# Idle products at the start, one weight piece a slot, another order of the value products, and later sums of weight factors

## The chip, the core and the metric

The kernel runs on one core of a Trainium2 chip. The metric is the device time of one execution in microseconds, as the median of several runs. The core's engines work side by side, each on its own queue in program order: TensorE (PE, matrix products), VectorE (DVE), ScalarE (ACT), GpSimd (POOL), and SyncE (SP), which here issues nearly all DMAs. Matmuls write to banks of PSUM; all other tiles lie in SBUF.

## What is computed

```python
def attn(q, k, v, g_q, g_k):                  # q, k, v: (8, 12, 448, 64)
    def rmsnorm(x, g):
        rms = np.sqrt(np.mean(x * x, axis=-1, keepdims=True) + 1e-06)
        return x / rms * g
    q_n, k_n = rmsnorm(q, g_q), rmsnorm(k, g_k)
    scores = np.matmul(q_n, k_n.transpose(0, 1, 3, 2)) / np.sqrt(64)
    scores = scores - np.max(scores, axis=-1, keepdims=True)
    attn = np.exp(scores)
    attn = attn / (np.sum(attn, axis=-1, keepdims=True) + 1e-09)
    return np.matmul(attn, v)

def moe(x, w_in, w_out):                      # (3584, 768), (768, 2048), (2048, 768)
    h = x @ w_in
    return (h - np.tanh(h)) @ w_out

# x = attention output, (B, H, S, D) -> (B*S, H*D)
```

The inputs w_in and w_out are float64; the kernel reads them as pairs of 32-bit words and rounds them to float32 itself.

## The kernel before

**Slots.** A step s is one batch and one pair of heads: 8 batches of NP = 6 pairs, 48 steps. The kernel is written out as a sequence of slots. Slot s holds the attention of step s, the scores of step s + 1, the turning (transposing) of q and k of step s + 2, the norms of step s + 3 and loads for later steps. `first_slot` (L958) writes slots -3 to 5, the first batch, in which there is no MLP to run beside it. `early_slot` (L995) writes slots 6 to 11 and `slot` (L1023) the rest; both call `run(gap)`, which takes so many nanoseconds of matmuls from one stream of MLP work of the batch before. Within an engine the order of the program is the order of execution; nothing is reordered by a planner.

**Attention.** `turn` (L427) transposes k and q on PE; ACT copies them to kT (with the gains, L434) and qT (L440). `scores(s, c)` (L507) makes the transposed scores of one chunk of keys (c = 0, 1, 2 are full chunks of 128 keys, c = 3 the rest of 64) and takes their exp on ACT (L527): chunks 0 and 1 go to tile p (two buffers), chunk 2 to p_full (one buffer), the rest to p_last. `totals` (L626) sums the exps over the keys with products by ones (L641) and takes the reciprocal on DVE (L646). `last_values` (L562, products L570) and `values` (L613, products L620) multiply by v into two PSUM banks; `divide` (L680) applies the reciprocal on DVE (L693) and, for the second half of a batch's pairs, forms sums of x for the MLP (L707 to L710, on POOL, for step 5 on DVE). Norms: ACT squares (L130, L131), DVE sums (L140, L141), POOL raises to the power -1/2 (L142), DVE scales q (L421). In a slot of the first batch PE goes through: scores of the next step (chunks 0, 1), turn, totals, scores of the rest, last_values, values, scores of chunk 2.

**MLP.** The matrix products of the MLP are made in blocks with a scheme of 7 products in place of 8 (`ORDER`, L179: factors 1, 5, 6, 2, 3, 7, 4). For w_in the 16 blocks of 128 columns form 4 sets j; a set has 7 products, and their weight factors are either rounded blocks (1, 2, 4) or sums and differences of such (5, 6, 3, 7). One product of the hidden layer is 6 matmuls of 128x128 by 128x224, L748. What DVE and ACT do with the products (adding up, tanh, L802 to L818) frees their three PSUM banks.

**Weights.** w_in and w_out come in 32 pieces of 768 KB (16 of w_in). `weight(to)` (L303) takes pieces up to number `to` one step further: ACT makes two passes over piece n (`round_weight_a`, L71 and L72), DVE three over piece n - 1 (`round_weight_b`, L78, L79, L82), POOL one over piece n - 1 (`round_weight_c`, L90), and SP loads a later piece (L272, L276). After the fourth piece of a set, `combine_weights` (L327) lists the set's four sums, and `combine(count)` (L333) makes so many of them on DVE (L335). In the first batch's MLP, `product` (L736) calls `weight(due[...])` and `combine(1)` ahead of each product and then makes any sum that the product needs. When a set's last sum is made, `keep_weights` (L340) can write its seven factors to DRAM, 7 x 384 KB, all on SP's queue (L343); this happens inside a later call of `weight`. The batches after the first read the factors from there. The tile that holds set 0's factors is later reused for set 3, and that of set 1 for w_out.

In `first_slot` a slot ends with

```python
        if s == -2:
            load_weights(2)
        else:
            weight(EARLY * (s + 3) // (NP + 2))
        combine(2)
```

With EARLY = 8 and NP = 6 this is `weight(2)` in slot -1 and `weight(s + 3)` in slots 0 to 5.

Of the kernel before, what the change touches and what calls it, by code (L numbers as in the profile page):

```python
# [9 lines left out]
F32 = mybir.dt.float32  # L10
# [5 lines left out]
PSUM = bass.MemoryType.PSUM  # L16
# [76 lines left out]
def fetch(nc, name, t, pair, in_order=False):  # L93

    S = pair.shape[1]
    P = 128
    KF, KR = S // P, S % P
    if name == "q":
        if in_order:
            for h in range(2):  # L100
                nc.sync.dma_start(out=t[:, h], in_=pair[h].rearrange("(c p) d -> p c d", c=NCH))
            return
        nc.sync.dma_start(
            out=t.rearrange("p h c d -> p h (c d)"), in_=pair.rearrange("h (p c) d -> p h (c d)", c=NCH)
        )
        return
    full, rest = pair[:, : KF * P].rearrange("h (p c) d -> h p c d", c=KF), pair[:, KF * P :]
    if name == "v":
        last = t[:, :, KF]
    elif in_order:  # L110
        last = t[:, KF]
    if in_order:
        for h in range(2):
            to = t[:, h, :KF] if name == "v" else t[:, :KF, h]
            nc.sync.dma_start(out=to, in_=pair[h, : KF * P].rearrange("(c p) d -> p c d", p=P))
    elif name == "v":
        nc.sync.dma_start(
            out=t[:, :, :KF].rearrange("p h c d -> p h (c d)"), in_=full.rearrange("h p c d -> p h (c d)")
        )
    else:  # L120
        last = t[:, KF]
        for h in range(2):
            nc.sync.dma_start(out=t[:, :KF, h], in_=full[h])
    for r in range(2):
        nc.sync.dma_start(out=last[r * KR : (r + 1) * KR], in_=rest.rearrange("h p d -> p h d"))  # L125


def squares_of(nc, sq, n, q, k):
# [16 lines left out]
def bounded_path(tc, ctx, q, k, v, moe_w_in, moe_w_out, out, g_col, ident, ones, half_ones, neg_half, early):  # L145
# [17 lines left out]
    nc = tc.nc  # L163
# [169 lines left out]
    def combine(count):  # L333
        for j, p, dst, x, y, op in combos[:count]:
            nc.vector.tensor_tensor(out=dst, in0=x, in1=y, op=op)  # L335
            if p == 7:
                kept[0] = j + 1
        del combos[:count]
# [88 lines left out]
    def turn(s, tk, tq):  # L427

        rr, n = normed.pop(s), early["n"]
        kn = loaded.pop(("k", s))  # L430
        for c in range(NCH):
            nc.tensor.transpose(tk[:, c * P : (c + 1) * P], kn[:, c].rearrange("p h d -> p (h d)"), ident)
        kT = qkp.tile([P, S], F32, name="kT")
        nc.scalar.mul(kT, tk[:, :S], g_col)  # L434
        for c in range(NCH):
            nc.tensor.transpose(
                tq[:, c * CP : (c + 1) * CP], n[:, c].rearrange("p h d -> p (h d)"), ident[:CP, :CP]
            )
        qT = qkp.tile([P, S], F32, name="qT")
        nc.scalar.copy(out=qT, in_=tq[:, :S])  # L440
        turned[s] = rr, kT, qT


# [96 lines left out]
    def full(s):  # L540

        return probs[s, 0][:, :, 0], probs[s, 1][:, :, 1], probs[s, 2][:, :, 0]

    def add(s):

        if s <= NP + NP // 2:
            sums[s] = []
            return
        t = early["sum"]
        sums[s] = [t]  # L550
        p = full(s)
        nc.vector.tensor_tensor(out=t, in0=p[0], in1=p[1], op=ALU.add)
        nc.vector.tensor_tensor(out=t, in0=t, in1=p[2], op=ALU.add)
# [56 lines left out]
        if has(s + 1):  # L610
            scores(s + 1, 2)

    def values(s, av):  # L613
        v_nat, p = loaded.pop(("v", s)), full(s)
        for n in range(2):
            for c in range(KF):
                for m in range(2):
                    for h in range(2):
                        r = (2 * m + h) * BL
                        nc.tensor.matmul(  # L620
                            av[n][r : r + BL, :HS], lhsT=v_nat[:, h, c, m * BL : (m + 1) * BL],
                            rhs=p[c][:, h, n * HS : (n + 1) * HS], start=False, stop=(c == KF - 1),
                        )
        return av

    def totals(s, dn):  # L626
# [86 lines left out]
    late = {}  # L713


    due = [EARLY + m // 2 + 1 for m in range(8)] + [12]
    due += [12 + m // 2 + 1 for m in range(8)]
    due += [CF + HF * (m + 1) // 11 for m in range(11)]
    assert len(due) == 7 * SETS and due[-1] == CF + HF
# [238 lines left out]
    def first_slot(s):  # L958

        if has(s + 1):  # L960
            scores(s + 1, 0)
            scores(s + 1, 1)
        if has(s + 2):
            turn(s + 2, mm_bank(), sc_bank())
        if s > -3:
            load(s + 4, "qk")
        if s > -3:
            squares(s + 3)
        norm(s + 3)
        if has(s):  # L970
            totals(s, mm_bank())
        if has(s + 2):
            load(s + 2, "v")
        if has(s + 1):
            scores(s + 1, KF)
        if has(s):
            av = [mm_bank() for _ in range(2)]
            last_values(s, av)
            values(s, av)
        if has(s + 1):  # L980
            scores(s + 1, 2)
            add(s + 1)
            add_last(s + 1)
        norm_q(s + 3)
        if s == -3:
            early["g_col"]()
        if has(s):
            divide(s, av)
        if s == -2:
            load_weights(2)  # L990
        else:
            weight(EARLY * (s + 3) // (NP + 2))
        combine(2)

    def early_slot(s):  # L995
        gap = gap_ns(s)
# [332 lines left out]
def kernel(  # L1329
# [42 lines left out]
    with tc.manual_schedule(), tc.tile_pool(name="g", bufs=1) as gp:  # L1372
        grow = gp.tile([1, 2, D], F32, name="grow")
        prod = gp.tile([1, D], F32, name="prod")
        nc.scalar.dma_start(out=grow[:, 0, :], in_=g_q[None, :])
        nc.scalar.dma_start(out=grow[:, 1, :], in_=g_k[None, :])
        for name, src in (("q", q), ("k", k)):
            fetch(nc, name, early[name], src[0, 0:2])
        for i, src in enumerate((g_q, g_k)):
            nc.sync.dma_start(out=gcol[:, i : i + 1], in_=src[:, None])  # L1380
        nc.vector.memset(warm, 0.0)
        nc.scalar.activation(warm, warm, AF.Exp)
        make_identity(nc, ident)
        nc.vector.memset(neg_half, -0.5)
        nc.vector.memset(ones, 1.0)
        nc.vector.memset(half_ones, 0.0)
        for i in range(2):
            nc.vector.memset(half_ones[i * D : (i + 1) * D, i], 1.0)
        nc.vector.tensor_tensor(out=prod, in0=grow[:, 0, :], in1=grow[:, 1, :], op=ALU.mult)
        nc.vector.tensor_tensor(out=prod, in0=prod, in1=prod, op=ALU.mult)  # L1390
        nc.vector.tensor_reduce(out=most, in_=prod, op=ALU.max, axis=AX.X)
        nc.vector.tensor_scalar(
            out=flag, in0=most, scalar1=(SCORE_MAX / (scale * D)) ** 2, scalar2=None, op0=ALU.is_le
        )
        squares_of(nc, early["sq"], early["n"], early["q"], early["k"])
        norm_of(nc, early["rr"], early["sq"], early["n"], neg_half)
# [47 lines left out]
```

## Time and profile before

| what | value |
|---|---|
| median of 3 runs | 1393.82 us (1392.56 to 1395.47) |
| the profiled execution's own time | 1394.93 us |
| its span | 1393.0 us |
| first totals (L641) of slots 0 to 5 start at | 20.89, 37.00, 46.52, 56.02, 66.19, 78.18 us |
| first product of the MLP (L748) starts at | 89.54 us |
| chain that ended last: PE's share | 87% |
| DMA | 249.91 MB, 179 GB/s on average |
| sums of factors (L335) | 16, 950 ns at least, 57.8 to 160.7 us |

How to read it: the span is from the first to the last instruction of the one execution that was profiled. Busy time of PE is that of pipelined matmuls, and a busy PE is not a PE at its peak. PEclk is the granted TensorE clock as a share of full speed. A line of the timeline has start and duration in us, engine, source line, operation, output and input tiles, shape and number of instructions; in square brackets is the time for which the engine stood idle before it and what ended this. A matmul of float32 shows as two records. Line numbers are those of the kernel before; below the inserted function they are 7 lower than in the changed kernel, and more further on.

### The profile page before, as it was taken

The page shows a single profiled execution, that of the slowest core. Times are in us where ns is not written, and L with a number is a line of the kernel's source. Part 1 is how long each engine was busy: PE and PEld are TensorE (multiplying, and loading weights), DVE is VectorE, ACT ScalarE, POOL GpSimd, SP SyncE. Part 2 cuts the span into 40 slices and gives each one's busy share as a digit, 9 for nine tenths or more (in the row PEclk, how much of TensorE's full clock was granted, in tenths as well). Part 3 has the DMA queues.
Part 4 walks back from the last instruction along what each step waited for, and adds up shares of the span by engine and source line. Part 5 has one row for each costly group of instructions (what it writes and reads, how often), then busy time and mean ns, then how long its engine had stood idle before and what let it go on. Part 6 is the DMA issues. An engine that isn't in the chain of part 4 may idle for free.

```text
span 1393.0 us, 29913 instructions
## 1 busy us (share of the span) xinstructions
PE 1358.7 (98%) x11840; PEld 1131.3 (81%) x11840; DVE 938.9 (67%) x1545; ACT 504.3 (36%) x1147; POOL 561.3 (40%) x345
## 2 busy tenths in 40 slices
PE   6999899999999999999999999999999999999997
PEld 2558664478898898889889988988988998899997
DVE  4799878856876688567867668657885677632311
ACT  5866555234422433233332343224333233301100
POOL 4565555314542346225544246423562255402310
PEclk9999999999999999999999999999999999999999
DMA  8769788766666766766666666666666667366663
GB/s 183 184 175 247 236 244 228 205 177 175 180 166 169 181 168 173 177 156 193 178 157 176 186 155 186 183 158 176 171 166 174 174 183 187 102 190 184 190 194 90
DMA packets 367657, 249.91 MB, mean 179 GB/s; under 512 B 281748, under 2 KB 309780, under 8 KB 367508
## 3 DMA queue, kind: packets, MB, share of 16 engines
q1 hardware_dynamic: 367504, 247.90, 66.4%
q8 instruction: 96, 1.57, 0.5%
q14 instruction: 53, 0.43, 0.1%
q10 hardware_dynamic: 4, 0.00, 0.0%
HBM read 214.40 MB, written 33.42 MB: 178 GB/s over the span
## 4 chain that ended last, share of the span: by engine, by line
PE 87%; DMA 4%; DVE 4%; ACT 1%; SPq 1%; issue 1%; POOL 0%; DVEq 0%; ACTq 0%
PE mm L748 66%; PE sc L521 8%; PE sc L582 6%; PE mm L913 4%; PE sc L570 1%; DMA w_f<-w_out 1%; DMA gT<-in_moe_w_in_dram 1%; PE sc L620 1%; DMA q_nat<-in_q_dram 1%; DMA w_raw<-in_moe_w_out_dram 1%; PE sc L641 1%; SPq L125 1%; DMA k_nat<-in_k_dram 0%; PE mm L620 0%; ACT p L527 0%
## 5 line engine op out<-in xcount | busy, mean ns | idle before, releaser
L748 PE MATMUL mm<-xT,w_f 128*128 128x224 f32 x1392 | 278.5, 355 | 1.7 <-DVE s L804 1.7
L748 PEld LDWEIGHTS mm<-xT,w_f 128*128 128x128 f32 x1392 | 261.3, 190 | 16.0 <-issue 10.2
L748 PEld LDWEIGHTS mm<-gT,w_f 128*128 128x128 f32 x1344 | 252.8, 191 | 12.8 <-issue 12.8
L748 PE MATMUL mm<-gT,w_f 128*128 128x224 f32 x1344 | 263.0, 354 | 0.0
L478 POOL TENSOR_TENSOR rr_mine<-rr_mine,neg_half 128x28 f32<-128x28 f32 x33 | 159.7, 4840 | 218.2 <-DVE rr_mine L477 218.2
L521 PE MATMUL sc<-qT,kT 64*32 64x448 f32 (+1 forms) x3072 | 216.4, 501 | 12.1 <-ACT p_last L527 8.3
L748 PE MATMUL mm<-tt,w_f 128*128 128x224 f32 x1044 | 208.8, 353 | 0.0
L748 PEld LDWEIGHTS mm<-tt,w_f 128*128 128x128 f32 x1044 | 197.0, 191 | 4.4 <-issue 4.4
L785 POOL TENSOR_TENSOR gT<-s,th 128x448 f32<-128x448 f32 x96 | 119.7, 1255 | 197.2 <-ACT th L784 190.6
L748 PE MATMUL mm<-tg,w_f 128*128 128x224 f32 x1008 | 197.5, 353 | 0.0
L748 PEld LDWEIGHTS mm<-tg,w_f 128*128 128x128 f32 x1008 | 190.7, 191 | 0.0
L521 PEld LDWEIGHTS sc<-qT,kT 64*32 64x32 f32 x3072 | 72.2, 107 | 82.3 <-issue 59.6
L686 DVE TENSOR_TENSOR xT<-xT,sc 128x448 f32<-128x448 f32 x35 | 21.8, 622 | 166.5 <-PE sc L521 110.8
L708 POOL TENSOR_TENSOR tt<-xT,tt 128x224 f32<-128x224 f32 x23 | 31.1, 1353 | 233.7 <-DVE xT L690 212.0
L665 ACT COPY sum_g<-sum 32x14 f32<-32x14 f32 x280 | 56.2, 201 | 186.5 <-DVE sum L657 173.0
L582 PE MATMUL sc<-p,v_nat 64*32 64x448 f32 x1120 | 110.5, 536 | 0.0
L784 ACT ACTIVATE th<-s 128x448 f32<-128x448 f32 x96 | 55.3, 577 | 115.3 <-DVE s L810 57.9
L527 ACT ACTIVATE p<-sc 128x448 f32<-128x448 f32 x132 | 71.7, 543 | 51.7 <-PE sc L521 39.1
L913 PE MATMUL mm<-gT,w_out 128*128 128x448 f32 x192 | 76.2, 553 | 0.3 <-POOL w_out L90 0.3
L913 PEld LDWEIGHTS mm<-gT,w_out 128*128 128x128 f32 x192 | 36.5, 195 | 38.2 <-issue 35.6
L582 PEld LDWEIGHTS sc<-p,v_nat 64*32 64x32 f32 x1120 | 40.7, 107 | 31.0 <-issue 31.0
L142 POOL TENSOR_TENSOR rr<-rr,neg_half 112x8 f32<-112x8 f32 (+1 forms) x30 | 49.7, 1680 | 38.1 <-DVE rr L141 38.0
(151 smaller groups left out, 1839.6 us busy)
## 6 DMA issues: line engine op xcount, KB each, us to landing
w_f<-w_in SPq DMA_DIRECT2D x196, 384.0 KB, 3.4
w_f<-w_out SPq DMA_DIRECT2D x147, 512.0 KB, 4.1
w_raw<-in_moe_w_out_dram SPq DMA_DIRECT2D x16, 768.0 KB, 5.0
out_dram<-th SPq DMA_DIRECT2D x192, 56.0 KB, 1.9
w_in<-w_out SPq DMA_DIRECT2D x21, 384.0 KB, 6.2
qk_nat<-in_q_dram SPq DMA_DIRECT2D x132, 56.0 KB, 2.6
qk_nat<-in_k_dram SPq DMA_DIRECT2D x132, 56.0 KB, 2.5
v_nat<-in_v_dram SPq DMA_DIRECT2D x72, 96.0 KB, 3.8
```

Source lines behind the costliest of these rows:

```text
L142: nc.gpsimd.tensor_tensor(out=r, in0=r, in1=neg_half[:rows], op=ALU.pow)
L478: nc.gpsimd.tensor_tensor(out=mine, in0=mine, in1=neg_half[:, :1].to_broadcast([P, 2 * NJ]), op=ALU.pow)
L521: nc.tensor.matmul(tiles[h][i * BL : (i + 1) * BL, :n], lhsT=kT[r, c * P + at : c * P + at + BL], rhs=qT[r, first : first + n], start=True ...
L527: nc.scalar.activation(p[:, h, c if c < 2 else 0, :], tiles[h][:, :n], AF.Exp, scale=1.0 if rr is None else rr[:, 0, 2 * c + h : 2 * c + h ...
L582: nc.tensor.matmul(av[g][i * BL : (i + 1) * BL, :S], lhsT=v_nat[keys, h, c, m * BL : (m + 1) * BL], rhs=p[keys, h], start=first, stop=True ...
L665: nc.scalar.copy(out=acc[h * BL : (h + 1) * BL, g], in_=part[g * BL : (g + 1) * BL, h * NJ : (h + 1) * NJ])
L686: nc.vector.tensor_tensor(out=x, in0=x, in1=av[1][:, :S], op=ALU.add)
L708: eng.tensor_tensor(out=t2, in0=x22, in1=t1, op=ALU.subtract)
L748: nc.tensor.matmul(bank[:, f * HS : (f + 1) * HS], lhsT=w[:, c * width + f, :], rhs=moving[p](c), start=(first and f == 0 and c == 0), sto ...
L784: nc.scalar.activation(th, h, AF.Tanh, bias=0.0, scale=1.0)
L785: eng.tensor_tensor(out=g[:, rows, cols], in0=h, in1=th, op=ALU.subtract)
L913: nc.tensor.matmul(bank[:, :S], lhsT=w_out_row(f, n // HC)[:, n % HC * P : (n % HC + 1) * P], rhs=g[:, f, :], start=(f == 0), stop=(f == C ...
```

## The change

- `keep_busy` is new. It issues products of the identity with its own first 64 columns; their result is not used. 12 stand on PE ahead of the branch at the start of the kernel, in a PSUM tile of their own; 18 stand in the turn of step 0 between the transposes of k and those of q, and 5 after those of q, in a bank that nothing else uses then.
- `values` goes through the chunks in the order 2, 0, 1 and, within a chunk, through the two halves of the queries; before, the halves were the outer loop and the chunks came as 0, 1, 2. In `first_slot` chunk 2 comes first, then the scores of chunk 2 of the next step, then the values of chunks 0 and 1. `early_slot` and `slot` call it for all three chunks.
- `first_slot` calls `weight(s + 2)` in place of `weight(s + 3)`: slot -1 takes piece 0 alone, and each later slot one piece. The first entries of `due` change from 9, 9, 10, 10, 11, 11, 12, 12 to 8, 9, 9, 10, 10, 11, 11, 12.
- `first_slot` no longer calls `combine(2)`. The sums of set 0 are made ahead of the MLP's products 0 to 3, those of set 1 ahead of products 4 to 7.
- From this follow moves on the queues: on SP the loads of pieces 3 and later come one slot later against the loads of q, k and v; the writing of set 0's factors moves from slot 4 to the sixth product of the MLP, behind the loads of pieces 11 and 12, and that of set 1 follows it after the loads of pieces 13 and 14. On ACT, DVE and POOL the passes over pieces 1 to 11 move by one place each; the number of instructions is the same but for the 35 idle products.

```diff
--- before.py
+++ after.py
@@ -125,6 +125,13 @@
         nc.sync.dma_start(out=last[r * KR : (r + 1) * KR], in_=rest.rearrange("h p d -> p h d"))
 
 
+def keep_busy(nc, ident, bank, count):
+
+    half = ident.shape[0] // 2
+    for _ in range(count):
+        nc.tensor.matmul(bank[:, 512 - half :], lhsT=ident, rhs=ident[:, :half], start=True, stop=True)
+
+
 def squares_of(nc, sq, n, q, k):
 
     nc.scalar.activation(n.rearrange("p c h d -> p (c h) d"), q.rearrange("p a b d -> p (a b) d"), AF.Square)
@@ -432,12 +439,16 @@
             nc.tensor.transpose(tk[:, c * P : (c + 1) * P], kn[:, c].rearrange("p h d -> p (h d)"), ident)
         kT = qkp.tile([P, S], F32, name="kT")
         nc.scalar.mul(kT, tk[:, :S], g_col)
+        if s == 0:
+            keep_busy(nc, ident, banks["mm"][0], 18)
         for c in range(NCH):
             nc.tensor.transpose(
                 tq[:, c * CP : (c + 1) * CP], n[:, c].rearrange("p h d -> p (h d)"), ident[:CP, :CP]
             )
         qT = qkp.tile([P, S], F32, name="qT")
         nc.scalar.copy(out=qT, in_=tq[:, :S])
+        if s == 0:
+            keep_busy(nc, ident, banks["mm"][0], 5)
         turned[s] = rr, kT, qT
 
 
@@ -610,17 +621,19 @@
         if has(s + 1):
             scores(s + 1, 2)
 
-    def values(s, av):
-        v_nat, p = loaded.pop(("v", s)), full(s)
-        for n in range(2):
-            for c in range(KF):
+    def values(s, av, chunks=(2, 0, 1)):
+        v_nat, p = loaded["v", s], full(s)
+        for c in chunks:
+            for n in range(2):
                 for m in range(2):
                     for h in range(2):
                         r = (2 * m + h) * BL
                         nc.tensor.matmul(
                             av[n][r : r + BL, :HS], lhsT=v_nat[:, h, c, m * BL : (m + 1) * BL],
-                            rhs=p[c][:, h, n * HS : (n + 1) * HS], start=False, stop=(c == KF - 1),
+                            rhs=p[c][:, h, n * HS : (n + 1) * HS], start=False, stop=(c == 1),
                         )
+        if 1 in chunks:
+            del loaded["v", s]
         return av
 
     def totals(s, dn):
@@ -713,7 +726,7 @@
     late = {}
 
 
-    due = [EARLY + m // 2 + 1 for m in range(8)] + [12]
+    due = [EARLY + (m + 1) // 2 for m in range(8)] + [12]
     due += [12 + m // 2 + 1 for m in range(8)]
     due += [CF + HF * (m + 1) // 11 for m in range(11)]
     assert len(due) == 7 * SETS and due[-1] == CF + HF
@@ -976,9 +989,12 @@
         if has(s):
             av = [mm_bank() for _ in range(2)]
             last_values(s, av)
-            values(s, av)
+            values(s, av, (2,))
         if has(s + 1):
             scores(s + 1, 2)
+        if has(s):
+            values(s, av, (0, 1))
+        if has(s + 1):
             add(s + 1)
             add_last(s + 1)
         norm_q(s + 3)
@@ -989,8 +1005,7 @@
         if s == -2:
             load_weights(2)
         else:
-            weight(EARLY * (s + 3) // (NP + 2))
-        combine(2)
+            weight(s + 2)
 
     def early_slot(s):
         gap = gap_ns(s)
@@ -1381,6 +1396,8 @@
         nc.vector.memset(warm, 0.0)
         nc.scalar.activation(warm, warm, AF.Exp)
         make_identity(nc, ident)
+        with tc.tile_pool(name="idle", bufs=1, space=PSUM) as idle:
+            keep_busy(nc, ident, idle.tile([P, 512], F32, name="idle"), 12)
         nc.vector.memset(neg_half, -0.5)
         nc.vector.memset(ones, 1.0)
         nc.vector.memset(half_ones, 0.0)
```

## The prediction

> **What bounds the kernel now.** I read the page's busy shares first, then the stretches of 20 us with busy time, clock and DMA share, then the timeline and the waits of the stretches in which PE is not full.
>
> ```profile
> PE 1358.7 (98%) x11840; PEld 1131.3 (81%) x11840; DVE 938.9 (67%) x1545; ACT 504.3 (36%) x1147; POOL 561.3 (40%) x345
> ...
> core 0: us, PE busy (x) PEld busy (x) DVE busy (x) ACT busy (x) POOL busy (x), PEclk, DMA share, GB/s
> 20.00:40.00 20.00, 16.39 (x236) 7.81 (x239) 9.48 (x17) 13.07 (x24) 8.41 (x5) 0.83 0.93 216
> 40.00:60.00 20.00, 19.50 (x356) 9.96 (x359) 16.60 (x28) 16.08 (x31) 10.31 (x6) 1.00 0.76 174
> 60.00:80.00 20.00, 16.70 (x285) 8.46 (x280) 19.48 (x28) 15.45 (x29) 15.27 (x13) 0.95 0.90 238
> 80.00:100.00 20.00, 19.98 (x233) 14.05 (x226) 19.52 (x27) 11.81 (x20) 11.31 (x7) 0.97 0.57 161
> 100.00:120.00 20.00, 20.00 (x225) 15.45 (x225) 19.57 (x30) 9.57 (x16) 11.54 (x8) 1.00 0.73 216
> 120.00:140.00 20.00, 20.00 (x183) 17.59 (x183) 18.59 (x24) 14.98 (x31) 11.29 (x8) 1.00 0.91 230
> ...
> 28.00:30.00 2.00, 2.00 (x28) 0.88 (x24) 1.48 (x4) 1.61 (x4) 0.58 (x1) 0.50 1.07 226
> ```
>
> PE is the bound over the whole span, so a gain can only come from its holes, nearly all before 300 us. The attention slots of the first batch run to 89.54 us (first L748). There PE idles or is slow at 20-40 (clock 0.50 from about 27.4 to 33.3 us) and at 60-80 (DVE 19.48 of 20). From 80 to 140 PE is full, but DVE is too: 57.68 of 60 us.
>
> ```profile
> 23.19 0.90 ACT L71 ACTIVATE w_out<-gT 128x768 f32<-128x768 f32 x1 [2.12 <-DMA gT<-in_moe_w_in_dram]
> ...
> 25.43 0.94 PE L521 MATMUL sc<-qT,kT 64*32 64x224 f32 x9 [2.82 <-ACT p L527]
> ...
> 53.45 1.16 ACT L527 ACTIVATE p_full<-sc,rr 128x448 f32<-128x448 f32 x2 [1.96 <-PE sc L521]
> ...
> 57.79 3.49 DVE L335 TENSOR_TENSOR w_out<-w_out,w_out 128x768 f32<-128x768 f32 x2
> ...
> 69.36 3.95 DVE L335 TENSOR_TENSOR w_out<-w_out,w_out 128x768 f32<-128x768 f32 x2
> ...
> 76.54 0.66 PE L432 MATMUL mm<-ident,k_nat 128*128 128x128 f32 x4 [2.42 <-DVE rs L646]
> ...
> 99.08 0.61 DVE L804 TENSOR_TENSOR s<-mm,s 128x448 f32<-128x448 f32 x1
> ...
> 170.72 1.74 PE L521 MATMUL sc<-qT,kT 64*32 64x448 f32 x14 [5.05 <-ACT p_last L527]
> ```
>
> The reader sees: ACT stands for the second weight piece's DMA, PE stands behind ACT, and the half clock follows; four sums of factors (7.44 us of DVE) end slots 2 and 3, and in the slots after them PE waits for DVE. By the first L641 of each slot, slots 1 to 5 begin at 37.00, 46.52, 56.02, 66.19, 78.18: 9.5 us where PE bounds, 10.2 and 12.0 where DVE does.
>
> **What the Trainium skill says.** "TensorE: Matmul & The Clock Gate", Part 1: the array starts at half clock, an idle window of about 3.4 us brings it back there, and about 3.4 us of activity releases it. The trace agrees in kind: 32 score matmuls take 3.11 us at 10.23 and 1.73 at 87.88; after the hole of 2.82 us the clock is 0.50 for some 6 us. "SBUF — State Buffer", Who interferes with whom: a DVE instruction with two SBUF inputs contends with a GpSimd one that reads SBUF. It agrees: L335 takes 950 ns at least, 1186 in the median, 2608 at most.
>
> **The change part by part.**
> *Idle products.* The 12 start when the identity is ready (1.30 us). The trace shows no such product: by moving columns an estimate from L748 (two records of 190 ns for 224 columns, so 109 ns for 64 columns at full clock); by weight loads two of 105 ns (L432: 0.42 us for 4). I take 0.21 us, twice this while cold. So 12 take 2.6 to 5.1 us and end at 4 to 6.5, beside the flag's computation (flag 4.26, PE's branch 5.1). The 18 between the transposes begin at about 6 and end at 9 to 11, where the q transposes start at 8.63 now: delay 0.5 to 2.5 us, less 0.4 for transposes at full clock. Slack for it is in slot -1: ACT waits for q_nat at 16.25 and k_nat at 17.06 (0.7 and 0.2 us). Taken: loss 0.5 (0 to 2). The 5 stand before scores that wait for qT: nothing. Their use is that PE is warm.
> *One piece a slot.* In slot -1 ACT went through piece 0 (to 21.07) and then stood for piece 1 to 23.19 and worked on it to 24.77. Now piece 1 comes a slot later, so the four exps start at 21.07: 3.7 us earlier, 3.1 of it on PE (scores at about 22.3 in place of 25.43; after that mm banks and kT). The hole of 2.82 goes, and with it the half clock: 6 us at half clock are 3.0 us lost. Its DMAs go a slot later too, so q and k of slot 4 are issued about 2 us earlier on SP; what is late next in slot 0 is the exps on ACT.
> *Third chunk first.* The same 48 products (2.41 us a slot) in another order. scores(s+1, 2) stands 1.6 us earlier, so p_full's exps run under the other values; ACT's 1.96 us of waiting goes, and kT, for which L570 waits 0.5 us a slot, comes earlier. Slots 1 to 4: 4 x 0.5 = 2.0. In slot 5 the denominators of slot 6 (2.32 us from 85.56) no longer wait for p_full: 1.65 as elsewhere, 0.7. In later slots p is complete anyway: nothing; divide's first half starts 1.2 us later, which only DVE feels.
> *Sums only in the MLP.* Four L335 (7.44 us) leave slots 2 and 3. Slot 3 falls from 10.17 to 9.5 (0.7), slot 4 from 11.99 to 9.5 (2.5), and the half-speed denominators of slot 5 (3.2 us in place of 1.65, after the hole) go: 1.5. What is late next is POOL in slots 3 and 4 (L142 3.24, L707 to L710 about 4, L90 1.86: 9.1 of 9.0 a slot), taken at 0.3 each.
> Sum up to the first L748: 3.1 + 3.0 + 2.0 + 0.7 + 0.7 + 2.5 + 1.5 - 0.6 - 0.5 = 12.4; I take 11.5, as the pieces overlap.
>
> *What it costs later.* The MLP's first products get the four sums and one piece (2.1 us of DVE: L78, L79, L82) more, in the stretch where DVE is full. Counted from the first L748 (T): DVE finishes slot 5's divide, L707 to L710 and its piece at T+1.3, L646 T+2.8, then piece, sum, piece, sum (2.1 + 1.4 + 2.1 + 1.4) to T+9.8 and L804 at T+10.4, where PE wants it at T+10.0 (today L804 ends 99.69, T+10.15). The fifth and sixth sums and two more pieces put the second L811 at T+25.3 against PE's need at T+23.8, and the set's last L818 and the next L806 2.5 to 3 us behind need. Each sum at 0.95 gives 1 us, at 2.0 gives 6. Taken: PE gives back 3.0 us in these products. From about 134 us DVE waits for PE today, so the lag ends there.
>
> *Moved DMAs.* Saving the first set (7 x 384 KB, SP 6.05 us to issue) moves from 73.9 us to the sixth product, behind the load that waits for L90, and the second save follows two loads later; pieces 13 to 15, q, k and v of the next slots queue behind both on SP.
>
> ```profile
> 94.00:104.00 10.00, 9.98 (x110) 8.41 (x112) 9.83 (x12) 6.09 (x11) 4.56 (x2) 1.00 0.01 2
> ...
> 114.00:122.00 8.00, 8.00 (x90) 5.83 (x89) 7.86 (x11) 4.88 (x13) 8.00 (x6) 1.00 1.04 387
> ...
> SPq L272 <- POOL w_f L90: 16.9, 3, 13.8
> ```
>
> A save drains at about 400 GB/s, 7 us of all queues, but it does not fall into the empty 10 us shown: SP stands there for a raw buffer. Piece 12 lands 4 us later than today against T, 13 to 15 1 to 5 us later; ACT waits before them with exps behind it. As PE itself is 3 us later, I take 0.5 (0 to 4). The hole at 165.7 (5.05 us for piece 20: its chain L78, L79, L82, L90, load starts from PE's order, which is the same) stays.
>
> Sum: 11.5 - 3.0 - 0.5 = 8.0. The profiled execution took 1394.93 (span 1393.0 and 1.9 around it), so 1386.9; it lies 1.1 above the median 1393.82, against which I say 1386.0.
>
> **Rivals.**
> (1) *DVE's lag is covered*: the sums run near 950 ns and L804's banks hold; 1393.8 - 12 = 1382. For: the DVE-bound slots leave no backlog at T. Against: 57.68 of 60.
> (2) *DVE is the bound to 134 us and takes all back*: in today's trace it is busy from 57.8 without a stop, and the change puts 2 us of idle into each of slots 3 to 5, which it must make up: 1391 to 1396. For: the shares. Against: it catches up by 134 today.
> (3) *The idle products run late or the clock halves anyway* (PE still idles some 2 us at 16-18): 3 to 4 us less, 1390.
> (4) *Slower: the two saves starve ACT of pieces 13 to 17.* Today's hole at 165.7 shows the price: 5.05 us, then half clock to about 177, 3 more, 8 us a hole. ACT waiting over 6 us at pieces 13 and 17 holds the exps so long that PE has two new holes: 16, plus 3 from DVE, less 11.5: 1401. It decides from where a piece lands 6 us past need. Against: each save is only 7 us of DMA.
>
> **How the numbers follow.** Forecast 0.50, (1) 0.17, (2) 0.15, (3) 0.06, (4) 0.12. About 0.2% (2.8 us) is what can be told from no change here. Faster: 0.50 + 0.17 + 0.05 + 0.04 of (2) = 0.76; same 0.07 of (2) + 0.01 = 0.08; slower 0.04 of (2) + 0.12 = 0.16. The range 1380 to 1396.5 leaves out (4) and a third of (1), 0.18.
>
> **What would show it.** First L748 at 76 to 80 us; no ACT wait at L71 near 22 us and clock 1.00 from 20 to 40; p_full's exps without a wait; slots of 9.0 to 9.3 us; DVE at 19.5 of 20 and PE waits for L804 to L818 of about 3 us within 40 us after T; the hole before p_last unchanged. First L748 later than 83, or a second hole of 5 us before 170, would make it wrong.

## The result and the profile after

The changed kernel takes 1395.45 us (median of 16 runs, 1394.45 to 1398.88) against 1393.84 (16 runs, 1390.09 to 1396.67) for the kernel before. The ratio is 1.0017, interval [1.0009, 1.0026]: slower by 0.17%. Of the 16 executions of the kernel after, eleven have a mean granted clock of 0.993 or 0.994 and take 1394.45 to 1395.66 us, five have 0.991 or 0.992 and take 1397.23 to 1398.88. The profiled execution is one of the eleven; its span is 1393.8 us, 0.8 more than that of before. The forecast was 1386.0.

So the 12 us that were to be gained ahead of the MLP left no trace in the total. The windows of 20 us show where to look (busy time of PE, weight loads, DVE, ACT and POOL with the number of instructions, granted clock, DMA share, GB/s):

```profile
core 0: us, PE busy (x) PEld busy (x) DVE busy (x) ACT busy (x) POOL busy (x), PEclk, DMA share, GB/s
20.00:40.00 20.00, 19.38 (x336) 8.83 (x324) 10.66 (x20) 19.32 (x37) 9.04 (x6) 1.00 0.73 175
60.00:80.00 20.00, 19.66 (x391) 9.95 (x388) 19.41 (x27) 17.08 (x31) 18.45 (x16) 1.00 0.85 196
80.00:100.00 20.00, 13.15 (x83) 11.00 (x68) 17.79 (x26) 8.66 (x15) 7.92 (x4) 0.83 0.53 116
120.00:140.00 20.00, 20.00 (x200) 15.94 (x181) 19.63 (x29) 14.95 (x30) 12.74 (x9) 1.00 1.02 334
160.00:180.00 20.00, 13.16 (x130) 9.10 (x129) 14.56 (x16) 12.23 (x20) 10.87 (x6) 0.83 0.75 223
```

The two bad windows of before, 20 to 40 and 60 to 80, are mended: PE is nearly full there and the clock is 1.00. In their place 80 to 100, which was full, now has 13.15 us of PE at a clock of 0.83. The window 160 to 180 was bad before (14.95 us of PE) and is worse. Two rows of PE's timeline carry these holes (start and duration in us, engine, line, operation, tiles, shape, count; in brackets the idle time before and what ended it):

```profile
90.81 5.87 PE L761 MATMUL mm<-tt,w_out 128*128 128x224 f32 x16 [6.85 <-DVE w_out L342]
...
174.56 1.74 PE L532 MATMUL sc<-qT,kT 64*32 64x448 f32 x14 [6.84 <-ACT p_last L538]
```

L342 is the sum of two factors (L335 before), L761 a product of the MLP (L748), L532 the scores (L521), L538 the exps (L527). The first hole is new: the MLP's second product waits for its weight factor, which is the first sum. After it, 16 records take 5.87 us where they take 3.19 elsewhere: the clock has halved. The second hole is the one before p_last, 5.05 us in the kernel before.

DVE's timeline says why the sum came so late. T, the start of the MLP's first product, is at 81.42 us:

```profile
80.69 1.62 DVE L706 TENSOR_TENSOR xT<-mm,rs 64x224 f32<-64x224 f32 x4
...
83.67 0.55 DVE L78 TENSOR_SCALAR w_out<-w_out 128x768 f32<-128x768 f32 x1
...
85.85 1.56 DVE L659 RECIPROCAL rs<-sc 128x224 f32<-128x224 f32 x1
87.32 0.88 DVE L78 TENSOR_SCALAR w_out<-w_out 128x768 f32<-128x768 f32 x1
...
89.71 0.95 DVE L342 TENSOR_TENSOR w_out<-w_out,w_out 128x768 f32<-128x768 f32 x1
90.58 2.19 DVE L78 TENSOR_SCALAR w_out<-w_out 128x768 f32<-128x768 f32 x1
```

At T, DVE is still at step 5's divide. Then come the sums of x, a weight piece, the reciprocal of the next step, a second piece, and only then the sum, at T + 8.3. PE asked for it at T + 2.5. And the start of the kernel, on PE:

```profile
1.36 5.39 PE L132 MATMUL idle<-ident 128*128 128x64 f32 x24 [1.36 <-POOL ident masks.py:199]
...
7.71 7.78 PE L132 MATMUL mm<-ident 128*128 128x64 f32 x36
15.28 0.95 PE L445 MATMUL sc<-ident,n 112*128 112x112 f32 x4
...
18.22 3.06 PE L532 MATMUL sc<-qT,kT 64*32 64x448 f32 x32
```

An idle product is two records of 216 to 225 ns (7.78 / 36 and 5.39 / 24), so 0.43 us or more, from the first to the last. The q transposes start at 15.28, 6.65 us later than before, the scores at 18.22, 8 us later. And after 17 us of this, with only the transposes of step 0 between them, the scores still take 3.06 us, as cold as before (3.11).

### The profile page after: what moved, and what is told of

It reads as the page before. It is cut to its first block, busy times and chain, and to the rows that moved or that the text cites. A ratio compares the mean times of both kernels' runs of the same rounds, so it can differ in the third digit from the quotient of the medians.

```text
span 1393.8 us, 30063 instructions
## 1 busy us (share of the span) xinstructions
PE 1365.7 (98%) x11910; PEld 1142.7 (82%) x11910; DVE 939.7 (67%) x1545; ACT 503.8 (36%) x1147; POOL 563.4 (40%) x345
## 4 chain that ended last, share of the span: by engine, by line
PE 88%; DMA 4%; DVE 4%; SPq 2%; issue 1%; ACT 1%; POOL 1%; DVEq 0%; POOLq 0%; ACTq 0%
PE mm L761 64%; PE sc L532 9%; PE sc L593 6%; PE mm L926 4%; DMA w_f<-w_out 1%; DMA w_raw<-in_moe_w_out_dram 1%; PE sc L581 1%; PE mm L631 1%; DMA w_raw<-in_moe_w_in_dram 1%; PE mm L132 1%; SPq L350 1%; PE mm L654 1%; DVE rs L659 1%; PE sc L631 1%; DVE w_out L82 0%
## 5 line engine op out<-in xcount | busy, mean ns | idle before, releaser
L761 PE MATMUL mm<-xT,w_f 128*128 128x224 f32 x1392 | 278.5, 354 | 1.7 <-DVE s L817 1.7
L761 PEld LDWEIGHTS mm<-xT,w_f 128*128 128x128 f32 x1392 | 261.3, 190 | 16.0 <-issue 10.2
L761 PEld LDWEIGHTS mm<-gT,w_f 128*128 128x128 f32 x1344 | 252.8, 190 | 12.8 <-issue 12.8
L761 PE MATMUL mm<-gT,w_f 128*128 128x224 f32 x1344 | 263.0, 354 | 0.0
L532 PE MATMUL sc<-qT,kT 64*32 64x448 f32 (+1 forms) x3072 | 216.0, 500 | 9.1 <-ACT p_last L538 8.8
L761 PE MATMUL mm<-tt,w_f 128*128 128x224 f32 x1044 | 208.7, 353 | 0.0
L761 PEld LDWEIGHTS mm<-tt,w_f 128*128 128x128 f32 x1044 | 197.0, 190 | 4.4 <-issue 4.4
L761 PE MATMUL mm<-tg,w_f 128*128 128x224 f32 x1008 | 197.5, 352 | 0.0
L761 PEld LDWEIGHTS mm<-tg,w_f 128*128 128x128 f32 x1008 | 190.7, 190 | 0.0
L532 PEld LDWEIGHTS sc<-qT,kT 64*32 64x32 f32 x3072 | 70.9, 106 | 77.1 <-issue 54.6
L538 ACT ACTIVATE p<-sc 128x448 f32<-128x448 f32 x132 | 71.9, 545 | 51.5 <-PE sc L532 39.0
```

What stands on the lines that cost most here:

```text
L532: nc.tensor.matmul(tiles[h][i * BL : (i + 1) * BL, :n], lhsT=kT[r, c * P + at : c * P + at + BL], rhs=qT[r, first : first + n], start=True ...
L538: nc.scalar.activation(p[:, h, c if c < 2 else 0, :], tiles[h][:, :n], AF.Exp, scale=1.0 if rr is None else rr[:, 0, 2 * c + h : 2 * c + h ...
L761: nc.tensor.matmul(bank[:, f * HS : (f + 1) * HS], lhsT=w[:, c * width + f, :], rhs=moving[p](c), start=(first and f == 0 and c == 0), sto ...
```

## The experiments

Five marks on PE serve for all kernels: the first scores, T, the first product of set 2 (the first that uses the w_f tile), the second layer's first product, and the next batch's first product of the MLP, all in us from the span's start. What lies behind the last mark is nearly the same in all, 1097.4 to 1098.0 us. Each mark is from one execution, and the executions of one kernel mostly spread over 2 to 7 us, so a difference of one or two us between two marks proves little by itself. The executions behind the marks of pool_sums and idle_stream were the slowest of their kernels, 2.2 and 2.7 us above the median.

The texts on record ahead of the runs name explanations by letters. A: the idle products cost start time, and what the sums cost depends only on where the first one stands. D: DVE's whole work up to about 130 us is the bound, wherever the sums stand. E: the hole before p_last comes from ACT standing for a weight piece. G: the shape of the idle products keeps the clock at half. B, C, F and H are rivals, each explained in its text.

| kernel | scores | T | set 2 | T to set 2 | second layer | next batch | median | ratio to before |
|---|---|---|---|---|---|---|---|---|
| before | 10.23 | 89.54 | 135.67 | 46.13 | 188.72 | 295.50 | 1393.84 | 1 |
| after | 18.22 | 81.42 | 137.72 | 56.30 | 191.18 | 295.81 | 1395.45 | 1.0017 [1.0009, 1.0026] |
| no_idle | 10.16 | 74.86 | 130.41 | 55.55 | 184.68 | 291.44 | 1391.06 | 0.9986 [0.9978, 0.9995] |
| idle_alone | 18.22 | 91.34 | 137.75 | 46.41 | 190.09 | 294.50 | 1393.41 | 1.0000 [0.9992, 1.0009] |
| sums_alone | 10.15 | 85.07 | 138.25 | 53.18 | 190.91 | 297.44 | 1396.92 | 1.0025 [1.0015, 1.0035] |
| piece_alone | 10.25 | 80.86 | 133.83 | 52.97 | 187.34 | 294.15 | 1392.36 | 0.9992 [0.9985, 0.9998] |
| chunk_alone | 10.02 | 86.61 | 133.77 | 47.16 | 186.61 | 293.46 | 1391.84 | 0.9985 [0.9974, 0.9995] |
| sums_back | 18.22 | 85.10 | 137.62 | 52.52 | 188.56 | 293.15 | 1393.35 | 1.0001 [0.9993, 1.0010] |
| no_idle_sums_back | 10.08 | 78.54 | 131.72 | 53.18 | 185.10 | 291.99 | 1390.23 | 0.9971 [0.9961, 0.9982] |
| pool_sums | 10.05 | 75.12 | 132.95 | 57.83 | 186.61 | 293.41 | 1390.49 | 0.9973 [0.9964, 0.9982] |
| no_sums0 | 10.07 | 76.30 | 125.77 | 49.47 | 180.00 | 287.00 | 1386.27 | 0.9947 [0.9933, 0.9961] |
| idle_stream | 13.22 | 76.14 | 132.06 | 55.92 | 186.52 | 292.79 | 1389.75 | 0.9978 [0.9968, 0.9987] |
| due_shift | 10.16 | 74.60 | 129.94 | 55.34 | 176.04 | 285.86 | 1385.75 | 0.9948 [0.9934, 0.9962] |
| early_sums_due | 10.15 | 79.30 | 132.17 | 52.87 | 176.25 | 286.13 | 1385.39 | 0.9933 [0.9920, 0.9947] |

Each ratio is against the kernel before on the same chip (medians 1393.24 to 1394.34).

### Undoing the idle products, the sums, or both

no_idle is the changed kernel without the three calls:

```diff
-        with tc.tile_pool(name="idle", bufs=1, space=PSUM) as idle:
-            keep_busy(nc, ident, idle.tile([P, 512], F32, name="idle"), 12)
...
-        if s == 0:
-            keep_busy(nc, ident, banks["mm"][0], 18)
...
-        if s == 0:
-            keep_busy(nc, ident, banks["mm"][0], 5)
```

sums_back keeps them and makes sums in the slots again; no_idle_sums_back does both:

```diff
             weight(s + 2)
+        combine(2)
```

> The changed kernel without its 35 idle products. Theory A (idle products cost start time; the late sum makes the hole): the first scores come 8 us earlier than in the changed kernel (10.2 in place of 18.2 us), all slots follow, the first product of the MLP starts at about 74 us, and the hole ahead of the second product stays at 6 to 9 us, as VectorE is as far behind as now. Time 1387 to 1390. Rival B (the idle products lay under loads): slot 0 still begins at 25 us or later, because q, k and the weight piece have not landed; gain under 3 us, 1393 or more. Rival C (the products keep the clock up): the clock halves in slots 0 or 1, and 3 us or more of the gain go, 1391 to 1393.

> The changed kernel with two sums of factors made at the end of each slot of the first batch again, as before the change; the rest as changed. Theory A: no wait for a sum ahead of the second product and no half clock there; slots 3 and 4 in time are bound by VectorE and take about 10 and 11 us in place of 8.7, so the first product of the MLP starts at 84 to 86 us; time 1389 to 1391. Rival D (VectorE's work up to 134 us is the bound wherever the sums stand): PE loses the same 8 to 10 us in the slots, and the time stays at 1394 to 1396.

> The changed kernel without idle products and with the sums made in the slots again, so that one weight piece a slot and the third chunk first are what is left of the change. Theory A: both gains add, 1382 to 1385. Rival B or D: 1390 or more.

Without the idle products T is 6.56 us earlier, the next batch 4.4 us, and the median 4.4 us: this is their price in the changed kernel. The clock is 1.00 from 20 to 40 us without them too, so they keep nothing warm that one piece a slot doesn't, and rival C falls. T and the hole (6.83 us) came as theory A had them; the time stayed above its 1390 us.

With the sums back in the slots the hole of 6.85 us is gone, but T comes 3.7 us later and four holes (1.2, 1.6, 2.5 us on this stretch and 1.9 ahead of it) stand in its place. The first product of set 2 is at 137.62 against 137.72: moving the sums back gains nothing there. Without idle products it is 131.72 against 130.41, and the median is 1390.23, where theory A wanted 1382 to 1385. Between the changed kernel and sums_back two effects nearly cancel. In the changed kernel DVE stands 3.1 us for PE behind the hole (four waits, 95 to 108 us), and in sums_back it has no wait over 0.2 us from 57 to 144 us; but set 0's four sums take it 7.9 us in the slots and 4.3 us in the MLP. So the late sum is how the loss shows; taking the hole away does not take the loss away.

### Each part alone, in the kernel before

idle_alone, sums_alone (`combine(2)` taken out), piece_alone (`weight(s + 2)` and the new first entries of `due`) and chunk_alone (the new order of the values):

> The kernel before with the 35 idle products alone. Theory A: the first scores come 8 us later; the wait for the second weight piece (until 23.2 us) hides a part, so 1397 to 1401. Rival B: hidden by loads, 1394 to 1395. The claim of the idle products (a clock that is up from the start): the half clock after 27 us goes, which gives 3 us back, 1391 to 1395. Measured by the way: whether the score products after the idle ones run at full speed (1.7 us for 32) or at half (3.1 us).

> The kernel before without the two sums at the end of each slot, the only edit: sums of set 0 are made ahead of the MLP's products. Theory D (VectorE's work from about 57 to 134 us is the bound, wherever in it the sums stand): slots 3 and 4 fall to 9.5 us and the MLP's first product comes 3 to 5 us earlier, at about 85; a hole of some 5 us opens ahead of the second product; the third set's first product starts at 136 to 138 us as before (135.7), time 1393 to 1396. Rival A (a gain in the slots is kept but for the hole): 1389 to 1391.

> The kernel before with one weight piece a slot and the due list shifted, the only edit; the two sums a slot stay. Both theories: the wait of ScalarE for the second piece and the half clock after it go, slot 0 falls from 16.1 to 9 to 10 us, and VectorE's work starts earlier by as much. Theory A: 6 us kept, 1387 to 1389. Theory D: VectorE starts its unbroken stretch about 5 us earlier but has a piece more in the MLP's first products (2.1 us) and pays that back: 1389 to 1391, most of what the pair without idle products gained.

> The kernel before with the third chunk's values ahead of the next scores, the only edit. Slots 1 and 2 take 8.7 to 9.0 us in place of 9.5, as ScalarE no longer waits for p_full's scores. Theory D: slots 3 and 4 are bound by VectorE and take the gain back; 1392.5 to 1394. Rival A: 2.0 us are kept, 1391 to 1392.

The idle products alone cost nothing: the scores come 8 us later, but the piece for which ACT stood in slot -1 has meanwhile landed. Of the hole of 2.82 us 0.38 are left, and the clock is 1.00 from 20 to 40 us, so T is only 1.8 us later and the total is the same. It is the one-piece edit that takes this cover away.

The sums are the part that is slower by itself. PE in sums_alone, at T and at the second product:

```profile
85.07 2.54 PE L748 MATMUL mm<-xT,w_out 128*128 128x224 f32 x12
92.59 3.70 PE L748 MATMUL mm<-tt,w_out 128*128 128x224 f32 x9 [4.98 <-DVE w_out L335]
```

T is 4.47 us earlier, nearly the 4.7 that the prediction had for it, and set 2 is 2.6 us later: 7.05 us more between the two. DVE, which has no wait over 0.2 us between 51 and 124 us in the kernel before, stands 4.2 us for PE here between 57 and 79 us (2.0, 1.2 and 1.0 us), and has the sums still to do.

chunk_alone came in at 1391.84 us, in the range of rival A and not in that of D, which had the gain taken back. Its trace shows what D's text left out: DVE's stretch without a wait begins at 48.38 us in place of 50.33, and set 2 comes 1.90 us earlier. What is gained before DVE is the bound stays gained. piece_alone gained less than either text had (1392.36 us): of 8.68 us at T, 1.84 are left at set 2.

### Is DVE the bound? Sums left out, and sums on GpSimd

no_sums0 fills the tiles of set 0's four sums with a constant; pool_sums makes the four on GpSimd at the end of slot 5. Both are without idle products.

```diff
         for j, p, dst, x, y, op in combos[:count]:
-            nc.vector.tensor_tensor(out=dst, in0=x, in1=y, op=op)
+            if j:
+                nc.vector.tensor_tensor(out=dst, in0=x, in1=y, op=op)
```

```diff
+        if s == NP - 1:
+            combine(4, nc.gpsimd)
```

> The changed kernel without the idle products, and without the four sums of set 0: their tiles are filled with a constant by GpSimd in slot 0, so the factors 5, 6, 3, 7 of the first two blocks of the hidden layer are left out in every batch. Theory D (VectorE's whole work to about 130 us is the bound): VectorE is spared some 5 us (0.95, 0.95, 2.07 and about 1), the hole near 84 us becomes 1 to 3 us elsewhere, and the first product of set 2 comes 4 to 6 us earlier, at 124.5 to 126.5 us against 130.4; theory E then takes part of it back before p_last: 1387 to 1389.5 us. Rival A (only the place of the first sum matters, VectorE has room otherwise): the first product of set 2 comes 46 us after the first product of all, as in the kernel before, at 121 us, and no idle of PE over 1 us stands between; 1382 to 1386. If VectorE isn't the bound at all: 130 and 1391, unchanged.

> The changed kernel without idle products, and with the four sums of set 0 on GpSimd, ahead of the last slot's piece; VectorE is rid of 4 to 7 us of work in its full stretch, and nothing else changes for it. Theory D: the third set's first product starts 4 to 6 us earlier than without idle products alone (130.4), the hole of 6.8 us ahead of the second product shrinks to under 2, the clock stays up, time 1385 to 1388. Rival E (the hole before p_last near 167 us, set by the weight pieces' loads, takes back what is gained ahead of it): the third set's first product comes earlier but the hole grows past 9 us, 1389 to 1391.

With DVE spared four sums, set 2 starts at 125.77 us, 4.64 earlier than in no_idle and inside what theory D said, although T comes 1.44 us later. Rival A wanted 121. DVE has no wait over 0.2 us from 30 to 132 us in this trace, so it is still full when set 2 starts. PE's timeline of no_sums0 shows that the waits for DVE are still there when no product waits for a sum:

```profile
78.68 3.19 PE L758 MATMUL mm<-tt,w_out 128*128 128x224 f32 x16
82.36 0.66 PE L440 MATMUL sc<-ident,k_nat 128*128 128x128 f32 x4 [0.49 <-DVE rs L656]
...
88.89 1.78 PE L758 MATMUL mm<-xT,w_out 128*128 128x224 f32 x8 [1.69 <-DVE s L814]
...
162.29 1.74 PE L529 MATMUL sc<-qT,kT 64*32 64x448 f32 x14 [6.53 <-ACT p_last L535]
```

The second part of the expectation failed: the hole before p_last did not take anything back (6.53 us against 6.71), and the median was 1386.27, under the range given.

pool_sums did not free DVE. While GpSimd made the sums

```profile
74.88 7.60 POOL L342 TENSOR_TENSOR w_out<-w_out,w_out 128x768 f32<-128x768 f32 x4
```

DVE's four sums of x beside them took up to five times as long as elsewhere (0.39 us each in the kernel after):

```profile
76.04 0.91 DVE L716 TENSOR_TENSOR tt<-xT 128x224 f32<-128x224 f32 x1
76.98 1.90 DVE L717 TENSOR_TENSOR tt<-xT,tt 128x224 f32<-128x224 f32 x1
78.81 2.02 DVE L718 TENSOR_TENSOR xT<-xT 128x224 f32<-128x224 f32 x1
80.74 1.99 DVE L719 TENSOR_TENSOR tt<-xT,tt 128x224 f32<-128x224 f32 x1
```

They lose 5.3 us, as much as the sums cost DVE in no_idle (4.9). The Trainium skill, "SBUF — State Buffer", Who interferes with whom, says that a VectorE instruction with two inputs in SBUF contends with a GpSimd instruction that reads SBUF, and calls the lock on the shared ports exclusive. The trace agrees: three of the DVE instructions last about as long as one sum on GpSimd (7.60 / 4 = 1.90). The hole only moved, to 86.43 us (5.75, for a reciprocal of DVE). Neither text came true: set 2 is 2.5 us later than in no_idle, and the hole before p_last did not grow (4.81 us).

### The hole before p_last

In the 20 us ahead of it ACT stands for weight pieces. Three rows of ACT in the kernel after:

```profile
150.00 0.96 ACT L71 ACTIVATE w_out<-w_raw 128x768 f32<-128x768 f32 x1 [1.53 <-DMA w_raw<-in_moe_w_out_dram]
159.89 0.90 ACT L71 ACTIVATE w_out<-w_raw 128x768 f32<-128x768 f32 x1 [4.11 <-DMA w_raw<-in_moe_w_out_dram]
...
172.48 0.91 ACT L71 ACTIVATE w_out<-w_raw 128x768 f32<-128x768 f32 x1 [3.77 <-DMA w_raw<-in_moe_w_out_dram]
```

The third is piece 20, and p_last's exps are queued behind it. due_shift is no_idle with one number changed, which puts that piece behind the exps of p_last and p_full:

```diff
+    due[23] = 20
     assert len(due) == 7 * SETS and due[-1] == CF + HF
```

> The changed kernel without the idle products, and one entry of the due list lowered from 21 to 20: ScalarE's two passes over weight piece 20 then stand behind the exps of p_last and p_full of the same slot instead of ahead of them; nothing else moves on PE, POOL or SP, and on DVE three passes (L78, L79, L82) move with it. Theory E (the hole of 6.7 us at 167 comes from ScalarE standing for the load of piece 20 with p_last's exps behind it): the exps run near 161.5 us, the hole shrinks to under 2 us, the half clock after it goes, and all later marks come 5 to 8 us earlier: about 1385 us (1383 to 1387.5), against 1391.1 without the shift. Rival F (the same load is only waited for at the next place: a later product of the set, or the next slot's exps, is late by as much): the hole turns up again within 20 us, 1389.5 to 1392.

ACT of no_idle and then of due_shift at this place:

```profile
164.99 0.91 ACT L71 ACTIVATE w_out<-w_raw 128x768 f32<-128x768 f32 x1 [3.56 <-DMA w_raw<-in_moe_w_out_dram]
165.80 0.93 ACT L72 ACTIVATE w_raw<-w_raw 128x768 int32<-128x768 uint32 x1
166.59 0.81 ACT L534 ACTIVATE p_last<-sc,rr 128x224 f32<-128x224 f32 x2
```

```profile
160.50 0.80 ACT L534 ACTIVATE p_last<-sc,rr 128x224 f32<-128x224 f32 x2
162.08 1.16 ACT L534 ACTIVATE p_full<-sc,rr 128x448 f32<-128x448 f32 x2 [0.77 <-PE sc L528]
164.28 0.92 ACT L71 ACTIVATE w_out<-w_raw 128x768 f32<-128x768 f32 x1 [1.04 <-DMA w_raw<-in_moe_w_out_dram]
```

The piece is processed at nearly the same time (164.28 against 164.99); only the exps no longer stand behind it, and they run 6.1 us earlier. PE's wait, in no_idle and then in due_shift:

```profile
167.12 1.75 PE L528 MATMUL sc<-qT,kT 64*32 64x448 f32 x14 [6.71 <-ACT p_last L534]
```

```profile
161.02 0.98 PE L528 MATMUL sc<-qT,kT 64*32 64x448 f32 x14 [1.09 <-ACT p_last L534]
```

It shrinks from 6.71 to 1.09 us, the second layer starts 8.64 us earlier, the next batch 5.6 us, and the median is 5.3 us lower. This is theory E, and its size. The shift was not tried in the kernel before. 3 us of the 8.64 are given back by the next batch: PE waits 2.02 us for POOL's gT up to 182.83, and the clock is 0.50 from 184 to 186 us behind it, where it is 1.00 at this place in no_idle.

### Idle products of another shape

idle_stream swaps what the idle products load and what they stream:

```diff
-        nc.tensor.matmul(bank[:, 512 - half :], lhsT=ident, rhs=ident[:, :half], start=True, stop=True)
+        nc.tensor.matmul(bank[:32, 384:], lhsT=ident[:, :32], rhs=ident, start=True, stop=True)
```

> The changed kernel with idle products of another shape: 32 columns of the identity as weights and 128 moving columns, in place of 128 weight columns and 64 moving ones; the count is the same 35. Theory G (what keeps the clock at half during the idle products is that the array mostly loads weights; streaming releases it): their records take about the same 216 ns at first and half of that later, the q transposes of step 0 start at 12 to 14 us in place of 15.3, and the first score products (x32) take 1.7 us in place of 3.06; 1392 to 1394 us. Rival H (the clock isn't released by idle products of any shape this early): the score products still take 3.1 us; 1394.5 to 1396.

```profile
1.36 5.33 PE L131 MATMUL idle<-ident 128*32 128x128 f32 x24 [1.36 <-POOL ident masks.py:199]
...
7.42 4.12 PE L131 MATMUL mm<-ident 128*32 128x128 f32 x36
11.47 0.60 PE L444 MATMUL sc<-ident,n 112*128 112x112 f32 x4
...
13.22 1.74 PE L531 MATMUL sc<-qT,kT 64*32 64x448 f32 x32
```

The first 24 records cost what they cost in the kernel after (5.33 against 5.39 us), but the next 36 take 114 ns each and not 216, the transposes 0.60 us and not 0.95, the scores 1.74 and not 3.06. The clock is released, as theory G had it, and the time is below its 1392. For the kernel it is worth the 5 us by which the scores come earlier than in the kernel after; against no idle products at all it gains nothing that the two medians can tell apart.

### Sums as early as their blocks allow

early_sums_due adds to due_shift: sum 7 behind piece 1, sum 5 behind piece 2, sum 6 behind piece 3, sum 3 in the MLP.

```diff
             weight(s + 2)
+            a = [built(0, p) for p in range(8)]
+            if s == 1:
+                combos.append((0, 7, a[7], a[1], a[0], ALU.subtract))
+                combine(1)
...
```

> The kernel with the shifted entry of the due list (no idle products), and set 0's sums made as soon as their blocks are rounded: sum 7 behind piece 1 at the end of slot 1, sum 5 behind piece 2 in slot 2, sum 6 behind piece 3 in slot 3, sum 3 at the first product of the MLP. Theory D (VectorE's whole work to about 130 us is the bound, and it has room only ahead of some 50 us): the hole of 6.8 us at the second product goes since sum 5 is there, the turn behind it waits instead; of the four sums about two fall where VectorE has idle time, so the first product of set 2 comes 1 to 3 us earlier than the 129.9 us of the kernel with the shifted entry, and the time is 1383 to 1385.5 against 1385.75. Rival A (the place of the first sum alone sets the loss): the first product of set 2 at 123 to 125 us, 1379 to 1382. A third case: the sums push VectorE's slots and PE waits for it in slots 4 and 5 as in the kernel before: first product of all later than 77 us and no gain, 1385 to 1388.

The third of the cases came. T is 79.30, and two of the sums made DVE stand, for the last pass over the piece just rounded, which GpSimd makes:

```profile
43.14 0.96 DVE L344 TENSOR_TENSOR w_out<-w_out,w_out 128x768 f32<-128x768 f32 x1 [2.03 <-POOL w_out L90]
...
53.65 0.96 DVE L344 TENSOR_TENSOR w_out<-w_out,w_out 128x768 f32<-128x768 f32 x1 [2.01 <-POOL w_out L90]
```

4 us of DVE go in waiting. PE's hole of 6.8 us at the second product is gone, but 1.0 to 1.1 us in each of two slots and 3.54 us at 93.59 (for L816 on DVE) stand in its place, and set 2 is 2.2 us later than in due_shift. No wait of PE over 0.4 us is left at this p_last, and the time is the same, 1385.39 against 1385.75. These two are the fastest complete kernels of the study, 0.5 to 0.7% faster than the kernel before.

## Why the prediction was wrong, point by point

**What held.** The gains ahead of T. The sum for them, idle products apart, was 12.4 + 0.5 = 12.9 us; no_idle has 14.7 (89.54 to 74.86). Part by part, alone in the kernel before: pieces 8.7 where 6.1 were written, the third chunk 2.9 where 2.0 + 0.7 were, the sums 4.5 where 0.7 + 2.5 + 1.5 were. They overlap, as the text said. Slots 1 to 3 take 8.7 us, below the 9.0 to 9.3 it expected, and slot 4 9.1. (The 32 score matmuls in its words on the clock are 32 records.) The hole of 2.82 us and the half clock after it are gone.

**Step that failed: "PE gives back 3.0 us in these products".** It gives back 9.4 without idle products (55.55 us from T to set 2 against 46.13), and 10.2 in the changed kernel. Two links in its working were wrong.

First, it set DVE at the end of slot 5's work and one piece at T + 1.3. In the kernel before that piece ends at 91.77, T + 2.2, and in no_idle at 79.24, T + 4.4. In the window 60 to 80 of the kernel after, PE's slots are 8.7 to 9.1 us long and DVE's work for one slot takes 9.8, by the reciprocals of slots 3, 4 and 5:

```profile
59.12 1.56 DVE L659 RECIPROCAL rs<-mm 128x224 f32<-128x224 f32 x1
...
68.94 1.56 DVE L659 RECIPROCAL rs<-mm 128x224 f32<-128x224 f32 x1
...
78.67 1.56 DVE L659 RECIPROCAL rs<-mm 128x224 f32<-128x224 f32 x1
```

So DVE falls behind before T. The prediction counted what leaves DVE's slots (7.44 us of sums), and did not check that slots which PE now does in 8.7 us leave DVE less time than it needs.

Second, its working dates the first sum at T + 4.9 to T + 6.3, and compares with PE's need only L804, at T + 10.0. But the second product of the MLP is product 5, and its factor is that sum: it was needed at T + 2.5. The order 1, 5, 6, 2, 3, 7, 4 was in the code before.

**What stood in its place** is rival (2), given 0.15: DVE is the bound to about 134 us and takes back what PE gains. It is shown by sums_alone (4.5 gained, 7.05 lost), by sums_back (set 2 no earlier without the hole) and by no_sums0 (DVE's work shortened, set 2 4.64 us earlier). It takes back most and not all: of 14.7 us at T, no_idle keeps 5.3 at set 2 and 4.1 at the next batch, and these the idle products then cost. The rival's words against it, "it catches up by 134 today", say when the lag ends; they do not show that PE is spared until then. The prediction's own sign of being wrong came too: a second hole of over 5 us before 170, that of 6.85.

**Idle products: "loss 0.5 (0 to 2)".** Measured 8.0 us at the first scores, 6.6 at T, 4.4 in the median. The duration was sized at 0.21 us, twice this while cold; all of them were cold, 0.43. The slack of slot -1 (ACT waiting for q and k, under 1 us) could not hide 8 us. The cover that did hide them, ACT's stand for piece 1, was taken away by the edit beside it: alone they cost nothing. And "their use is that PE is warm" was wrong for this shape. The first half of rival (3), idle products that run late, came true; its half clock did not (1.00 from 20 to 40 us).

**"The hole at 165.7 stays".** It stayed and grew, 5.05 to 6.84 us. The ground given, that its chain starts from PE's order, left out that ACT's own queue makes the hole: one place in that queue is worth 5.3 us. How much of the growth is due to the saves, now issued between 115 and 135 us (DMA share 1.02 and 1.03 in the windows from 120 to 160), was not tried.

**Rival (4)**, starving ACT, did not decide: from 115 to 175 us its waits ahead of pieces are 3.9 (for the first save itself, which has to read the tile before piece 12 is written there), 2.2, 5.5, 1.5, 4.1 and 3.8 us, none over 6, and the only hole of PE that comes from them is the old one.

By the marks, the kernel after is 8.1 us ahead at T, 2.05 behind at set 2, 2.5 behind at the second layer and 0.3 behind at the next batch. The last 2.2 us come back near 242 us, at a wait for p_last: it is 1.93 us in the kernel before, and the clock is 0.50 from 242 to 244 us and 0.70 for the next two; it is 1.47 us in the kernel after, and the clock stays at 1.00. The three kernels with the first shape of idle products take 104.4 to 104.6 us between these two marks, the others 106.3 and more; whether the idle products have to do with that clock was not tried.

## What to carry to other kernels

When PE's stage is made shorter, hold each other engine's work per slot against the new slot length, not against the old: the one that needs more than PE arrives at the next stage with a backlog, and the gain is lent, not given. For work that is moved later, date it against its first consumer in the program's own order, before dating anything behind it. A wait that an in-order engine cannot avoid costs only what is queued behind it, so look first at the queue: here one changed number was worth 5.3 us in the kernel without idle products, while the four edits together lost 1.6.

## What the runs showed of the hardware

- Idle products of 128 weight columns and 64 moving columns kept PE busy without a stop for 17 us and left it at half speed; with 32 weight columns and 128 moving columns (records of 222 ns at first, 114 later) it was released within some 6 us of their start. The Trainium skill, "TensorE: Matmul & The Clock Gate", Part 1, says that about 3.4 us of activity do this. That agrees with the second shape in kind, and not with the first: here it was not enough that PE was busy. The shapes differ in two numbers, so which of them decides was not separated, and weight loading as the reason is not shown.
- The clock column of the profile shows 1.00 in both kernels from the start, while records take twice their later time. In the first 20 us the durations tell the state, and the column does not.
- Half speed follows a hole of 6.85 us (16 records in 5.87 us and not 3.19), as it followed one of 2.82 us in the kernel before. Shorter holes went both ways at the same place in the program: 1.37 us at 238 us in idle_stream was followed by a clock of 0.50 from 240 to 242 us, 1.47 us at 243 us in the kernel after was not. So the length of a hole alone did not decide it.
